# Transposing the split local probabilities by VectorE and DMAs through DRAM

## The chip, the cores and the metric

One core of a Trainium2 chip runs the whole program. The metric is the device time of one execution in microseconds (us); the time of a kernel is the median of its runs. The core has a matrix engine (TensorE, PE in the profile, with its weight loads as PEld), three engines for elementwise work (VectorE or DVE, ScalarE or ACT, GpSimd or POOL) and SP, which in this program only issues DMAs. Each engine takes its instructions in the order in which they stand in its row; between the rows semaphores order the work.

## What is computed

Eight sequences of 512 tokens, each with 32 global tokens, go through attention with 8 heads of 64 columns, and the result through a gated feed-forward network (FFN). A local token attends to the 32 global tokens and to the local ones at most 32 positions away. A global token attends to all 544.

```python
k_all = np.concatenate([k_g, k_l], axis=2)
v_all = np.concatenate([v_g, v_l], axis=2)
out_g = np.matmul(sm(scale * np.matmul(q_g, k_all.transpose(0, 1, 3, 2))), v_all)
mask = np.abs(pos[:, None] - pos[None, :]) <= 32
s_ll = np.where(mask, scale * np.matmul(q_l, k_l.transpose(0, 1, 3, 2)), -1000000000.0)
s_lg = scale * np.matmul(q_l, k_g.transpose(0, 1, 3, 2))
out_l = np.matmul(sm(np.concatenate([s_lg, s_ll], axis=-1)), v_all)
x = np.concatenate([out_g, out_l], axis=2)   # as (8 * 544) x 512
gate = 1.0 / (1.0 + np.exp(-(x @ w_gate)))
return (gate * (x @ w_val) @ w_out).astype(np.float32)
```

`sm` is the softmax over the last axis; `w_gate` and `w_val` are 512 x 1536, `w_out` is 1536 x 512.

## The kernel before

**Number format.** The matrix products keep float32 accuracy by splitting: a tensor is cast to `float32r` (the high part), the high part is subtracted from it (the low part), and a product is made from high times high, low times high and high times low. ScalarE makes the casts, GpSimd or VectorE the subtractions.

**The two streams.** `ffn_stream` (L370) emits the FFN, chunk after chunk: two chunks of 256 tokens, seven of 512 and one for the global tokens. Each of a chunk's 12 items has 12 products into `bank_g`, 12 into `bank_v` and 12 into the four output banks, in groups of four 512-column products. After each group it yields, which is one step of the clock `now`. `att_events` (L428) lays the attention of a chunk on this clock as events with due times, and the main loop (L526 to L529) emits each event when its time has come. A 512-token chunk has 108 groups, and in them runs the attention of the next chunk: 8 heads, 12 groups apart, the first `BASE` = 3 groups after the start of the chunk.

**A head.** It has two local units of two blocks of 128 queries each and one global unit, `PER` = 4 groups apart. `load_qk` (due 16 groups ahead) and `load_v` load `qk_raw` and `v_raw`, `split_qk` (10 ahead) casts `qk_raw` to `qk_hi` on ScalarE and makes the key's low part `kl` and the query's low part (in place) on GpSimd (L183 to L186). `qk_raw` has one buffer, `qk_hi` and `kl` two.

**A local unit** (`local_unit`, L211) is a generator whose parts come 0, 3, 6 and 9 groups after its due time (`STAGES`, L39):

1. scores of both blocks into one PSUM bank (L229, each block high by high and high by low), the row maximum and mask on VectorE (L241), the exponential and its sum on ScalarE (L244). The window of a block has 192 or 224 columns. The unit of blocks 2 and 3 also has the global tokens' scores among themselves (L223).
2. the reciprocal of the sum and the scaling (L252 to L255, L208)
3. the transpose of the probabilities by TensorE: four products with the identity, two a block (L264, L265: columns 0 to 127, and the last 128), into one more PSUM bank, then the split: the cast from PSUM to `pt` by ScalarE (L274) and the subtraction by VectorE (L275)
4. the products with the values (L294, L295), the sum of their parts (L297 to L299)

Units of the first two chunks and of half the third are `native`: they have no split (24 of 128 units; 104 are split).

**What sets the order.** The code hands instructions to a scheduler in the order of the events, and it makes the row of each engine, moving an instruction back where its inputs or buffers are not ready by its own estimate. In the kernel before the products of nearly all units stand 9 groups behind their scores in TensorE's row, as the due times ask. PSUM has four banks under the tag `att`, which scores, transposes, products, `bank_g` and `bank_v` share in turn. All DMAs go through SP's one row: the loads, `wo` (the split `w_out`, one load an item, two buffers, L405) and the results (`out_dram`, L423, from `ob`).

**The start.** The first chunk's units are mixed with matmuls on constants (`warm`, L199) that nobody reads.

## Time and profile before

| | us |
|---|---|
| median of 3 runs (lowest, highest) | 1208.36 (1205.93, 1217.74) |
| profiled execution | 1206.77 |
| its span, first to last instruction | 1204.7 |
| mean granted TensorE clock | 0.987 |

The profile is one execution. A span is shared out over engines and lines; a busy time counts an engine's instructions, whether or not another engine waits for them. What TensorE's share means is read from the starts of its instructions, since the ends of matmuls are modelled. The stretches of 128 us below are about one batch's FFN each, with the attention of the next batch in it up to 1033 us (columns: stretch, its length, busy time and count of PE, PEld, DVE, ACT and POOL, granted clock, busy share of the DMA engines, GB/s):

```profile
0.00:60.00 60.00, 51.97 (x318) 39.49 (x318) 41.03 (x136) 42.07 (x118) 20.22 (x35) 1.00 0.72 248
60.00:160.00 100.00, 86.23 (x514) 67.71 (x515) 74.22 (x189) 71.65 (x190) 42.39 (x35) 0.85 0.69 230
...
520.00:648.00 128.00, 127.49 (x700) 106.02 (x699) 85.76 (x280) 89.18 (x201) 72.16 (x78) 1.00 0.38 114
...
1033.00:1150.00 117.00, 117.00 (x535) 95.89 (x534) 26.39 (x49) 37.86 (x73) 24.69 (x24) 1.00 0.21 72
```

The first 160 us, with the conversion of the weights in them, have TensorE's gaps and a lower clock; from there to the end it is busy nearly without a gap, and the DMA engines are a third busy.

### The profile page before, as it was taken

The page shows a single profiled execution, that of the slowest core. Times are in us where ns is not written, and L with a number is a line of the kernel's source. Part 1 is how long each engine was busy: PE and PEld are TensorE (multiplying, and loading weights), DVE is VectorE, ACT ScalarE, POOL GpSimd, SP SyncE. Part 2 cuts the span into 40 slices and gives each one's busy share as a digit, 9 for nine tenths or more (in the row PEclk, how much of TensorE's full clock was granted, in tenths as well). Part 3 has the DMA queues.
Part 4 walks back from the last instruction along what each step waited for, and adds up shares of the span by engine and source line. Part 5 has one row for each costly group of instructions (what it writes and reads, how often), then busy time and mean ns, then how long its engine had stood idle before and what let it go on. Part 6 is the DMA issues. An engine that isn't in the chain of part 4 may idle for free.

```text
span 1204.7 us, 19673 instructions
## 1 busy us (share of the span) xinstructions
PE 1172.4 (97%) x6606; PEld 971.4 (81%) x6606; DVE 727.5 (60%) x2275; ACT 780.2 (65%) x1836; POOL 585.4 (49%) x631
## 2 busy tenths in 40 slices
PE   8887999999999999999999999999999999999998
PEld 7565778888888888888888888888888888888897
DVE  5866874756776567756765677757775677511121
ACT  6766786767677677767766767767776776532232
POOL 2442553645656366545656465636654565311111
PEclk9978899999999999999999999999999999999999
DMA  7674763433334433333334433443434332131143
GB/s 259 237 270 166 253 210 105 118 120 112 98 103 130 125 105 123 97 127 105 115 97 123 125 95 110 127 128 100 128 97 127 106 114 75 53 105 55 68 145 119
DMA packets 50277, 152.80 MB, mean 127 GB/s; under 512 B 6144, under 2 KB 7168, under 8 KB 50176
## 3 DMA queue, kind: packets, MB, share of 16 engines
q1 hardware_dynamic: 50176, 151.54, 40.2%
q8 instruction: 52, 0.85, 0.3%
q14 instruction: 49, 0.40, 0.1%
HBM read 136.31 MB, written 15.20 MB: 126 GB/s over the span
## 4 chain that ended last, share of the span: by engine, by line
PE 75%; ACT 8%; DVE 7%; issue 6%; POOL 2%; DMA 1%; SPq 0%; POOLq 0%; ACTq 0%; DVEq 0%
PE bank_g L385 20%; PE bank_o L414 19%; PE bank_v L385 18%; PE bank_x L229 5%; PE bank_x L330 3%; PE bank_x L294 2%; PE bank_y L264 2%; PE bank_y L265 2%; PE bank_x L295 2%; ACT s_buf L244 1%; PE bank_x L308 1%; DVE s_buf L208 1%; ACT pg_buf L343 1%; POOL hh L401 1%; PE bank_x L288 1%
## 5 line engine op out<-in xcount | busy, mean ns | idle before, releaser
L385 PE MATMUL bank_g<-xt,wg 128*128 128x512 f32 (+1 forms) x1440 | 337.2, 369 | 1.0 <-ACT xt L367 0.9
L385 PE MATMUL bank_v<-xt,wv 128*128 128x512 f32 (+1 forms) x1440 | 329.1, 364 | 0.0
L414 PE MATMUL bank_o<-wo,hh 128*128 128x512 f32 x1224 | 325.0, 399 | 0.3 <-ACT hh L400 0.2
L385 PEld LDWEIGHTS bank_g<-xt,wg 128*128 128x128 f32 x1440 | 239.6, 191 | 41.6 <-issue 3.0
L385 PEld LDWEIGHTS bank_v<-xt,wv 128*128 128x128 f32 x1440 | 236.3, 188 | 38.0 <-issue 1.1
L414 PEld LDWEIGHTS bank_o<-wo,hh 128*128 128x128 f32 x1224 | 219.2, 189 | 41.7 <-issue 1.1
L401 POOL TENSOR_TENSOR hh<-th,hh 128x512 fp32r<-128x512 f32 (+1 forms) x120 | 136.7, 1139 | 237.8 <-ACT hh L400 226.8
L397 DVE SCALAR_TENSOR_TENSOR bank_v<-ex,bank_v 128x512 f32<-128x512 f32 (+1 forms) x120 | 73.1, 610 | 152.1 <-PE bank_v L385 148.7
L184 POOL TENSOR_TENSOR kl<-qk_raw,qk_hi 128x736 fp32r<-128x736 f32 x52 | 92.2, 1773 | 132.9 <-ACT qk_hi L183 131.8
L244 ACT ACTIVATE s_buf<-s_buf,nm 128x192 f32<-128x192 f32 (+1 forms) x248 | 114.1, 461 | 50.2 <-DVE nm L241 47.8
L400 ACT CAST hh<-th 128x512 fp32r<-128x512 f32 (+1 forms) x120 | 66.6, 555 | 115.4 <-DVE th L398 114.7
L393 ACT ACTIVATE th<-bank_g 128x512 f32<-128x512 f32 (+1 forms) x120 | 63.4, 528 | 83.5 <-PE bank_g L385 82.6
L241 DVE CUSTOM_DVE_ANT_0 s_buf<-bank_x,masks 128x192 f32<-128x192 f32 (+1 forms) x248 | 82.3, 367 | 41.9 <-PE bank_x L229 40.4
L299 POOL TENSOR_TENSOR x<-t 64x256 f32<-64x256 f32 x104 | 77.0, 740 | 62.0 <-DVE t L298 59.4
L196 POOL TENSOR_TENSOR vhl<-v_raw,vhl 128x512 fp32r<-128x512 f32 x52 | 67.0, 1288 | 47.8 <-ACT vhl L195 45.8
L208 DVE TENSOR_SCALAR s_buf<-s_buf,r 128x224 f32<-128x224 f32 (+1 forms) x230 | 86.1, 396 | 3.8
L183 ACT CAST qk_hi<-qk_raw 128x1280 fp32r<-128x1280 f32 x52 | 65.8, 1266 | 29.1 <-PE bank_x L308 17.8
L275 DVE TENSOR_TENSOR pt<-bank_y,pt 128x512 fp32r<-128x512 f32 x104 | 71.5, 687 | 20.6 <-ACT pt L274 20.0
L298 DVE TENSOR_TENSOR t<-bank_x,t 64x512 f32<-64x512 f32 x104 | 70.7, 680 | 21.0 <-ACT t L297 17.3
L186 POOL TENSOR_TENSOR qk_hi<-qk_raw,qk_hi 64x256 fp32r<-64x256 f32 x104 | 78.8, 772 | 4.7
L252 DVE TENSOR_SCALAR r<-sm 128x2 f32<-128x2 f32 x128 | 33.5, 262 | 78.2 <-ACT s_buf L244 78.2
L398 DVE SCALAR_TENSOR_TENSOR th<-th,bank_v 128x512 f32<-128x512 f32 (+1 forms) x120 | 72.4, 603 | 6.1 <-DVE bank_v L397 0.5
(117 smaller groups left out, 2003.1 us busy)
## 6 DMA issues: line engine op xcount, KB each, us to landing
wo<-wo_dram SPq DMA_DIRECT2D x116, 512.0 KB, 3.3
qk_raw<-in_qk_dram SPq DMA_DIRECT2D x104, 320.0 KB, 4.6
v_raw<-in_v_dram SPq DMA_DIRECT2D x52, 256.0 KB, 2.6
out_dram<-ob SPq DMA_DIRECT2D x34, 256.0 KB, 3.0
xt<-in_w_gate_dram SPq DMA_DIRECT2D x12, 512.0 KB, 4.5
xt<-in_w_val_dram SPq DMA_DIRECT2D x12, 512.0 KB, 4.1
xt<-in_w_out_dram SPq DMA_DIRECT2D x12, 512.0 KB, 4.2
v_nat<-in_v_dram SPq DMA_DIRECT2D x8, 512.0 KB, 3.9
```

Of the source, the lines that this page charges most:

```text
L184: nc.gpsimd.tensor_tensor(kl, t[:, K0:Q1], hi[:, K0:Q1].bitcast(F32), op=ALU.subtract)
L186: nc.gpsimd.tensor_tensor(hi[64:128, r], t[64:128, r], hi[64:128, r].bitcast(F32), op=ALU.subtract)
L208: nc.vector.tensor_scalar(out, in_, by, None, op0=ALU.mult)
L241: anchor[0] = nc.vector.tensor_tensor_reduce(out=s_sb[:, i, 0:w], in0=s_ps[:, i, 0:w], in1=masks[:, m:m + w], scale=-0.125, scalar=3.0e38, ...
L244: nc.scalar.activation(s_sb[:, i, 0:w], s_sb[:, i, 0:w], AF.Exp, bias=nm[:, i:i + 1], scale=-1.0, accum_out=sm[:, i:i + 1])
L275: nc.vector.tensor_tensor(pt[:, 1], pt_ps, pt[:, 0].bitcast(F32), op=ALU.subtract)
L299: nc.gpsimd.tensor_tensor(dst, t0[:, :, 0], t0[:, :, 1], op=ALU.add)
L385: nc.tensor.matmul(acc, w[a][:, t, fs], xt[:, c, t, x0:x0 + ntok], start=n == 0, stop=n == 11)
L397: nc.vector.scalar_tensor_tensor(acc, ex, 1.0, acc, op0=ALU.min, op1=ALU.mult)
L398: nc.vector.scalar_tensor_tensor(th, th, 1.0, acc, op0=ALU.add, op1=ALU.mult)
L401: nc.gpsimd.tensor_tensor(hh[:, 1, 0:ntok], th, hh[:, 0, 0:ntok].bitcast(F32), op=ALU.subtract)
L414: nc.tensor.matmul(o_ps[t], ph[:, a, t * P:(t + 1) * P], pwo[:, c], start=f2 == 0 and i == 0, stop=f2 == NF - 1 and i == 2)
```

## The change

The 104 split units no longer use TensorE for step 3. VectorE transposes each 32x32 block of the two blocks' 224 columns (`tb`: 7 column blocks, 2 query blocks, 32 columns). Four DMAs, one for each 32 partitions, write it to a scratch in DRAM, `pd`, in runs of 64 numbers (256 bytes). Two DMAs read it back as 128 rows of 256 numbers each: rows 0 to 127 of the window, and rows 96 to 223. The result lies in SBUF, in the place of the low part; ScalarE casts it to the high part, and the subtraction, in place, goes to GpSimd for a head's first unit (blocks 0 and 1) and to VectorE for its second. The products read the same numbers, in runs of 32 columns.

The due times follow: writes stay at 3 groups, the reads come 5.5 groups behind them, the cast and subtraction 9, the products 11.5 (14.5 after the scores, which was 9), and `BASE` goes from 3 to -2, so that attention starts 5 groups earlier. For `ob` there are three buffers instead of four, and the warm-up uses the identity alone, twice as many products of half as many columns.

```diff
-BASE, PER = 3, 4
+BASE, PER = -2, 4
 STAGES = (0, 3, 6, 9)
+STAGES_DMA = (5.5, 9, 11.5)
...
-            nc.tensor.matmul(bank[:, 0:256], ident_r, masks_r, start=True, stop=True)
+            nc.tensor.matmul(bank[:, 0:P], ident_r, ident_r, start=True, stop=True)
...
-            s_sb = ffn.tile([P, 2, WIN], F32, name="s_first", tag="ob", bufs=4)
+            s_sb = ffn.tile([P, 2, WIN], F32, name="s_first", tag="ob", bufs=3)
...
-            pt = att.tile([P, 2, 4, P], F32R, name="pt", bufs=2)
-            nc.scalar.copy(pt[:, 0], pt_ps)
-            nc.vector.tensor_tensor(pt[:, 1], pt_ps, pt[:, 0].bitcast(F32), op=ALU.subtract)
+            tb = att.tile([P, 7, 2, 32], F32, name="tb", bufs=2)
+            pd = dram.tile([7, 32, 4, 64], F32, name="pd", bufs=3)
+            nc.vector.transpose(tb.rearrange("p b k i -> p k b i"), s_sb.rearrange("p k (b i) -> p k b i", i=32))
+            for a in range(4):
+                rows = slice(32 * a, 32 * a + 32)
+                nc.sync.dma_start(pd[:, :, a].rearrange("b j r -> j b r"), tb[rows].rearrange("p b k i -> p b (k i)"))
+            yield
+            pt = att.tile([P, 2, 2, 4, 2, 32], F32R, name="pt", bufs=2)
+            for m in range(2):
+                src = pd[3 * m:3 * m + 4].rearrange("b j a r -> (b j) (a r)")
+                nc.sync.dma_start(pt[:, 1, m].rearrange("p a k i -> p (a k i)").bitcast(F32), src)
+            yield
+            flat = pt.rearrange("p c m a k i -> p c (m a k i)")
+            nc.scalar.copy(flat[:, 0], flat[:, 1].bitcast(F32))
+            (nc.vector if blocks[0] else nc.gpsimd).tensor_tensor(
+                flat[:, 1], flat[:, 1].bitcast(F32), flat[:, 0].bitcast(F32), op=ALU.subtract)
...
-            nc.tensor.matmul(o_ps[:, i], vt[:, VM[j], :], pt[:, :, 2 * i, :], start=True, stop=False)
-            nc.tensor.matmul(o_ps[:, i], vt[0:sides[i], VS[j], :], pt[0:sides[i], :, 2 * i + 1, :], start=False, stop=True)
+            out = o_ps[:, i].rearrange("p c (a i) -> p c a i", i=32)
+            nc.tensor.matmul(out, vt[:, VM[j], :], pt[:, :, 0, :, i, :], start=True, stop=False)
+            nc.tensor.matmul(out, vt[0:sides[i], VS[j], :], pt[0:sides[i], :, 1, :, i, :], start=False, stop=True)
...
-                            ob = ffn.tile([P, DM], F32, name="ob", bufs=4)
+                            ob = ffn.tile([P, DM], F32, name="ob", bufs=3)
...
+            steps = STAGES if T["native"] else (0, 3) + tuple(3 + o / sc for o in STAGES_DMA)
```

The rows of the engines change with it. In the changed kernel L308 and L309 are the products that were L294 and L295, L399 and L428 the FFN's. TensorE's row in the steady part, before: the products of a unit (of values `vhl` and probabilities `pt`), a group of four FFN products, the transposes of another unit, a group.

```order
L294 MATMUL bank_x<-pt,vhl 128x256
L295 MATMUL bank_x<-pt,vhl 128x256
L294 MATMUL bank_x<-pt,vhl 128x256
L295 MATMUL bank_x<-pt,vhl 128x256
L385 MATMUL bank_v<-xt,wv_119 128x512 x4
L264 MATMUL bank_y<-ident,s_buf_108 128x128
L265 MATMUL bank_y<-ident,s_buf_108 128x128
L264 MATMUL bank_y<-ident,s_buf_108 128x128
L265 MATMUL bank_y<-ident,s_buf_108 128x128
L385 MATMUL bank_v<-xt,wv_118 128x512 x4
```

And in the changed kernel: the products of a head's first unit, right behind them the scores of the next head's second unit (L223 stands in front of those alone), then FFN groups and the products of the second unit.

```order
L308 MATMUL bank_x<-pt,vhl 128x256
L309 MATMUL bank_x<-pt,vhl 128x256
L308 MATMUL bank_x<-pt,vhl 128x256
L309 MATMUL bank_x<-pt,vhl 128x256
L223 MATMUL bank_x<-qk_hi 32x32
L223 MATMUL bank_x<-kl,qk_hi 32x32
L229 MATMUL bank_x<-qk_hi 128x224
L229 MATMUL bank_x<-kl,qk_hi 128x224
L229 MATMUL bank_x<-qk_hi 128x192
L229 MATMUL bank_x<-kl,qk_hi 128x192
L399 MATMUL bank_g<-xt,wg_114 128x512 x4
L399 MATMUL bank_g<-xt,wg_115 128x512 x4
```

The transposes are gone from the row, the products stand 12 to 19 groups behind their unit's scores, and a head's first product has the next head's second scores at its back.

SP's row over two heads, before: only loads (`qk_raw` and `v_raw` of a head to come, `wo` of an FFN item).

```order
L159 DMA qk_raw<-in_qk_dram 64x1280 x2
L405 DMA wo<-wo_dram_124 128x1024
L174 DMA v_raw<-in_v_dram 128x512
L159 DMA qk_raw<-in_qk_dram 64x1280 x2
L405 DMA wo<-wo_dram_125 128x1024
```

SP's row for one head and the start of the next in the changed kernel: the writes of both units, the loads of `qk_raw`, the reads of the first unit, `wo`, the reads of the second.

```order
L278 DMA pd<-tb 32x7x64 x8
L159 DMA qk_raw<-in_qk_dram 64x1280 x2
L283 DMA pt<-pd 128x256 x2
L419 DMA wo<-wo_dram_120 128x1024
L283 DMA pt<-pd 128x256 x2
L174 DMA v_raw<-in_v_dram 128x512
L278 DMA pd<-tb 32x7x64 x4
```

The loads of `qk_raw` and the first unit's reads moved behind the second unit's writes, which wait for VectorE.

GpSimd's row for a head, before: the split of the queries and keys of a head to come in one piece (`kl`, then `qk_hi` twice), then the FFN's low part `hh`.

```order
L184 TENSOR_TENSOR kl<-qk_raw,qk_hi 128x736
L186 TENSOR_TENSOR qk_hi<-qk_raw,qk_hi 64x256
L186 TENSOR_TENSOR qk_hi<-qk_raw,qk_hi 64x288
L401 TENSOR_TENSOR hh<-th,hh 128x512
L360 TENSOR_TENSOR ptg<-ptg_buf,ptg 128x5x32
```

In the changed kernel (L287 is the subtraction in `pt`, L313 the last sum of a unit's result):

```order
L184 TENSOR_TENSOR kl<-qk_raw,qk_hi 128x736
L287 TENSOR_TENSOR pt<-pt 128x512
L186 TENSOR_TENSOR qk_hi<-qk_raw,qk_hi 64x256
L186 TENSOR_TENSOR qk_hi<-qk_raw,qk_hi 64x288
L313 TENSOR_TENSOR x_5325<-t_5521 64x256
```

The subtraction of a head's first unit came in behind the `kl` of a head to come, which needs the `qk_raw` just loaded.

More of the change, by code (lines that the diff above doesn't have):

```diff
@@ L83 @@
     nc.scalar.copy(masks[:, WIN + P + 32:WIN + 192], masks[:, P + 64:WIN])
-    ident_r, masks_r = (const.tile([P, w], F32R, name=nm) for w, nm in ((P, "ident_r"), (256, "masks_r")))
+    ident_r = const.tile([P, P], F32R, name="ident_r")
     nc.scalar.copy(ident_r, ident)
-    nc.scalar.copy(masks_r, masks[:, 0:256])
     s_bufs = [const.tile([P, 2, WIN], F32, name=f"s_buf{i}") for i in range(3)]
@@ L216, in local_unit @@
         if T["first"]:
-            warm(s_ps.rearrange("p a c -> p (a c)"), 16 if h == 0 else 2)
+            warm(s_ps.rearrange("p a c -> p (a c)"), 32 if h == 0 else 4)
         with_gg = T["with_g"] and blocks[-1] == 3
@@ L255, in local_unit @@
             scaled(nat, s_sb[:, i, 0:KWIN[j]], s_sb[:, i, 0:KWIN[j]], r[:, i:i + 1])
-        yield
-        if T["first"]:
-            pt_ps = ps.tile([P, 4, P], F32, name="bank_y", tag=f"bank_o{h % 2}")
-            warm(pt_ps.rearrange("p a c -> p (a c)"), 2)
-        else:
-            pt_ps = ps.tile([P, 4, P], F32, name="bank_y", tag="att", bufs=4)
         sides = [KWIN[j] - (WIN - P) for j in blocks]
-        for i in range(2):
-            nc.tensor.transpose(pt_ps[:, 2 * i], s_sb[:, i, 0:P], ident)
-            nc.tensor.transpose(pt_ps[:, 2 * i + 1], s_sb[:, i, WIN - P:WIN], ident)
         if nat:
+            yield
+            if T["first"]:
+                pt_ps = ps.tile([P, 4, P], F32, name="bank_y", tag=f"bank_o{h % 2}")
+                warm(pt_ps.rearrange("p a c -> p (a c)"), 4)
+            else:
+                pt_ps = ps.tile([P, 4, P], F32, name="bank_y", tag="att", bufs=4)
+            for i in range(2):
+                nc.tensor.transpose(pt_ps[:, 2 * i], s_sb[:, i, 0:P], ident)
+                nc.tensor.transpose(pt_ps[:, 2 * i + 1], s_sb[:, i, WIN - P:WIN], ident)
             if T["first"] and h % 2:
@@ L272, in local_unit @@
         else:
-            pt = att.tile([P, 2, 4, P], F32R, name="pt", bufs=2)
-            nc.scalar.copy(pt[:, 0], pt_ps)
-            nc.vector.tensor_tensor(pt[:, 1], pt_ps, pt[:, 0].bitcast(F32), op=ALU.subtract)
+            tb = att.tile([P, 7, 2, 32], F32, name="tb", bufs=2)
[9 more added lines that the diff above has]
+                nc.sync.dma_start(pt[:, 1, m].rearrange("p a k i -> p (a k i)").bitcast(F32), src)
+            yield
+            flat = pt.rearrange("p c m a k i -> p c (m a k i)")
+            nc.scalar.copy(flat[:, 0], flat[:, 1].bitcast(F32))
+            (nc.vector if blocks[0] else nc.gpsimd).tensor_tensor(
+                flat[:, 1], flat[:, 1].bitcast(F32), flat[:, 0].bitcast(F32), op=ALU.subtract)
         yield
@@ L464, in att_events @@
             ev.append((base - sc * SPLIT_V, 1, lambda T=T: split_v(T)))
+            steps = STAGES if T["native"] else (0, 3) + tuple(3 + o / sc for o in STAGES_DMA)
             for i in range(npu):
                 t0 = base + per * i
-                for o in STAGES if i < nu else (0, 3, 3.9) if T["native"] else (0, 3):
+                for o in steps if i < nu else (0, 3, 3.9) if T["native"] else (0, 3):
                     ev.append((t0 + sc * o, 2, lambda h=h, i=i: adv(h, i)))
             if h % 2 == 1:
-                ev.append((base + (nu - 1) * per + sc * STAGES[-1] + 0.5, 3,
+                ev.append((base + (nu - 1) * per + sc * steps[-1] + 0.5, 3,
                            lambda kt=h // 2: x_split(xts[ci], x32s[kt], kt, x0, ntok)))
```

## The prediction

> **What bounds the kernel now.** I read the page first: the busy shares, then the chain that ended last.
>
> ```profile
> PE 1172.4 (97%) x6606; PEld 971.4 (81%) x6606; DVE 727.5 (60%) x2275; ACT 780.2 (65%) x1836; POOL 585.4 (49%) x631
> ...
> PE 75%; ACT 8%; DVE 7%; issue 6%; POOL 2%; DMA 1%; SPq 0%; POOLq 0%; ACTq 0%; DVEq 0%
> PE bank_g L385 20%; PE bank_o L414 19%; PE bank_v L385 18%; PE bank_x L229 5%; PE bank_x L330 3%; PE bank_x L294 2%; PE bank_y L264 2%; PE bank_y L265 2%; PE bank_x L295 2%; ACT s_buf L244 1%; PE bank_x L308 1%; DVE s_buf L208 1%; ACT pg_buf L343 1%; POOL hh L401 1%; PE bank_x L288 1%
> ```
>
> TensorE is idle for 32 us of 1204.7 us, so its instructions are the time: two lines of transposes, L264 and L265, hold 4% of the chain. Since a busy PE here is modelled, I then looked at start times in a steady stretch (start, duration, engine, line).
>
> ```profile
> 599.73 0.87 PE L385 MATMUL bank_g<-xt,wg 128*128 128x512 f32 x3
> 600.44 0.27 PE L264 MATMUL bank_y<-ident,s_buf 128*128 128x128 f32 x1
> 600.55 0.27 PE L265 MATMUL bank_y<-ident,s_buf 128*128 128x128 f32 x1
> 600.66 0.27 PE L264 MATMUL bank_y<-ident,s_buf 128*128 128x128 f32 x1
> 600.76 0.27 PE L265 MATMUL bank_y<-ident,s_buf 128*128 128x128 f32 x1
> 600.79 1.19 PE L385 MATMUL bank_g<-xt,wg 128*128 128x512 f32 x4
> 601.82 1.09 PE L385 MATMUL bank_v<-xt,wv 128*128 128x512 f32 x4
> 602.75 0.25 PE L229 MATMUL bank_x<-qk_hi 128*128 128x192 f32 x1
> ...
> 603.19 1.10 PE L385 MATMUL bank_v<-xt,wv 128*128 128x512 f32 x4
> 604.13 0.28 PE L294 MATMUL bank_x<-pt,vhl 128*128 128x256 f32 x1
> 604.24 0.28 PE L295 MATMUL bank_x<-pt,vhl 128*128 128x256 f32 x1
> 604.36 0.28 PE L294 MATMUL bank_x<-pt,vhl 128*128 128x256 f32 x1
> 604.48 0.28 PE L295 MATMUL bank_x<-pt,vhl 96*128 96x256 f32 x1
> ...
> 617.47 0.25 PE L229 MATMUL bank_x<-qk_hi 128*128 128x192 f32 x1
> ```
>
> A group of four FFN matmuls takes 604.13 - 603.19 = 0.94 us. From 599.73 to 601.82 seven of them and four transposes take 2.09 us; less 7 x 0.235 that leaves 0.44 us for a unit's transposes. One head (two local units and a global one among twelve groups) takes 617.47 - 602.75 = 14.72 us.
>
> **What goes.** 104 units lose their transposes: 104 x 0.44 = 46 us of TensorE. If all else hides, 1206.8 (the profiled execution; the median of the runs, 1208.4, is 1.6 us above it) becomes 1161. A head would then take 14.72 - 2 x 0.44 = 13.84 us.
>
> **What comes, engine by engine.**
>
> ```profile
> L401 POOL TENSOR_TENSOR hh<-th,hh 128x512 fp32r<-128x512 f32 x84 | 108.5, 1292 | 171.4 <-ACT hh L400 164.9 <-DMA qk_raw<-in_qk_dram 5.1
> L184 POOL TENSOR_TENSOR kl<-qk_raw,qk_hi 128x736 fp32r<-128x736 f32 x52 | 92.2, 1773 | 132.9 <-ACT qk_hi L183 131.8 <-ACT xg L311 1.1
> L275 DVE TENSOR_TENSOR pt<-bank_y,pt 128x512 fp32r<-128x512 f32 x104 | 71.5, 687 | 20.6 <-ACT pt L274 20.0
> L298 DVE TENSOR_TENSOR t<-bank_x,t 64x512 f32<-64x512 f32 x104 | 70.7, 680 | 21.0 <-ACT t L297 17.3
> L183 ACT CAST qk_hi<-qk_raw 128x1280 fp32r<-128x1280 f32 x52 | 65.8, 1266 | 29.1 <-PE bank_x L308 17.8 <-PE bank_x L330 10.9
> L357 DVE STREAM_TRANSPOSE ptg_buf<-pg_buf 32x128 f32<-32x128 f32 x208 | 62.8, 302 | 3.4
> L297 ACT COPY t<-bank_x 64x512 f32<-64x512 f32 x104 | 59.7, 574 | 2.0 <-PE bank_x L295 0.6
> L354 DVE STREAM_TRANSPOSE ptg_buf<-pg_buf 32x32 f32<-32x32 f32 x52 | 10.5, 201 | 4.1 <-ACT pg_buf L343 2.3
> ```
>
> VectorE: the block transpose has 448 columns. From 32 to 128 columns the rows grow by 101 ns, 1.05 ns a column, so about 0.64 us: 104 x 0.64 = 67 us. The subtraction (0.69 us) stays there for 52 units, so VectorE changes by 67 - 36 = +31 us, to some 63% of the span. GpSimd gets 52 subtractions of 1.29 us, +67 us. ScalarE's copy reads SBUF in place of PSUM, about the same. None of these is the bound as a sum.
>
> SP gets six DMAs a unit, 624 in all, and the DMA engines 1152 packets a unit (896 of 256 bytes, 256 of 1 KB), 50 MB.
>
> ```profile
> DMA packets 50277, 152.80 MB, mean 127 GB/s; under 512 B 6144, under 2 KB 7168, under 8 KB 50176
> ...
> q1 hardware_dynamic: 50176, 151.54, 40.2%
> ```
>
> That is 40.2% x 16 x 1204.7 us / 50176 = 154 ns for a mean packet of 3.0 KB. No row has data packets of 256 bytes. By bytes they add 50/151.5 x 40.2 = 13% of the engines' time; at the mean packet's price 119,808/50176 x 40.2 = 96%. I take 25%, near the byte end, since the mean packet is twelve times as large.
>
> The Trainium skill ("DMA: Bandwidth & Descriptors", Specifications) says that transfers under 512 B are done by read-modify-write and miss line rate. No run here shows it. By that rule the 256-byte writes lie nearer the other end, which is the second rival.
>
> **The wait that I think decides.** On TensorE the scores of a head's second unit stand right behind the product of the head before's first unit (the order under the change). Those scores feed the transpose on VectorE, this feeds four writes on SP, and behind them in SP's row stand the two loads of `qk_raw`, then the reads of `pt`. On GpSimd, `kl` (from that `qk_raw`) stands ahead of the first unit's subtraction, for which TensorE waits. So each product waits for the one before it through a loop over five engines and DRAM. First VectorE's part of it in a steady stretch, then SP's issues (start, time of issue), then `qk_raw` from issue to landing, its median and its spread:
>
> ```profile
> 608.57 0.37 DVE L241 CUSTOM_DVE_ANT_0 s_buf<-bank_x,masks 128x224 f32<-128x224 f32 x1
> ...
> 610.92 0.57 DVE L208 TENSOR_SCALAR s_buf<-s_buf,r 128x224 f32<-128x224 f32 x2
> ```
>
> ```profile
> 533.63 2.04 SPq L423 DMA_DIRECT2D out_dram<-ob  x4
> ...
> 602.56 0.34 SPq L174 DMA_DIRECT2D v_raw<-in_v_dram  x1
> 604.44 1.11 SPq L159 DMA_DIRECT2D qk_raw<-in_qk_dram  x2
> ```
>
> ```profile
> qk_raw<-in_qk_dram SPq DMA_DIRECT2D x104, 320.0 KB, 4.6
> ```
>
> ```profile
> DMA to landing us min/median/max: 3.6/4.6/7.6
> ```
>
> - product on TensorE, 604.13 to 604.76: 0.63
> - its copy and sum (L297, L298), which VectorE does ahead of the next reduction: 1.25
> - reduction to scaled probabilities, 608.57 to 611.49: 2.92
> - block transpose: 0.64
> - four issues: 1.3 (v_raw's 0.34 each) to 2.0 (the four stores); I take 1.7
> - `qk_raw`: its second issue starts 0.55 later and lands 4.6 after that (3.6 at least): 5.15
> - cast, `kl`, subtraction: 1.27 + 1.77 + 1.29 = 4.33
>
> The writes wait for the transpose on SP, and `wo` is queued behind them too:
>
> ```profile
> SPq L405 <- PE bank_o L414: 416.2, 78, 11.5
> ```
>
> SP sits waiting for a free `wo` buffer up to 11.5 us, so `wo` has slack for that; `qk_raw` is the load in the loop. Behind a product that waits, TensorE's FFN groups wait as well, since it takes its row in order.
>
> Sum of the loop: 16.6 us, against 13.84 us of TensorE's work in a head of twelve groups; with the shortest rows 15.2.
>
> Counted in the order, the groups from second scores to first product are 13, 12, 15, 9, 12.25, 14.75, 12 and 9 for the eight heads of a batch: 14.8, 13.8, 16.7, 11.0, 14.1, 16.4, 13.8 and 11.0 us. Five heads (second to sixth) have the full loop; the first, seventh and eighth have no `kl` close ahead, which leaves some 12.5 us (14 in the first, behind the stores). TensorE then lacks 2.8 (second), 5.6 (fourth), 2.5 (fifth), 0.2 (sixth) and 1.5 us (eighth): 12.6 a batch, 76 us over the six batches that run so.
>
> A wait that long also costs clock. Before (start, duration, and the idle time ahead in brackets; then a stretch with its granted clock behind the busy times):
>
> ```profile
> 107.11 0.43 PE L348 MATMUL bank_y<-ident,pg_buf 32*128 32x32 f32 x4 [2.80 <-ACT pg_buf L343]
> ...
> 121.57 0.63 PE L348 MATMUL bank_y<-ident,pg_buf 32*128 32x32 f32 x4 [2.92 <-ACT pg_buf L343]
> ```
>
> ```profile
> 120.00:130.00 10.00, 8.43 (x48) 7.83 (x49) 7.65 (x13) 6.14 (x16) 6.42 (x5) 0.66 0.84 275
> ```
>
> Around gaps of 2.8 and 2.9 us the clock falls to 0.66 over ten us, 3.4 us of full speed lost. The fourth head's 5.6 us exceeds both. Its 3.4 us go into a head that lacked 2.5 us anyway, so I add 0.9 x 6 = 5 us.
>
> The Trainium skill ("TensorE: Matmul & The Clock Gate", Part 1) puts the drop at an idle window of about 3.4 us. The trace agrees in kind. By the skill's figure the second head's 2.8 us trips nothing and the sum below stands; by the trace's gaps it is at the edge, and if it trips each time the sum is 6 x 3.4 = 20 us more, 1262.
>
> **Small edits.** The warm-up matmuls keep their columns (16 x 256 = 32 x 128) but double their loads, and a ScalarE copy ahead of them goes: between minus 3 and plus 8 us at the start, taken as nothing. Three `ob` tiles for four: the fourth result waits for the first store, with some 7 us until its bank is written again; nothing, and at most 3 us a batch if the stores land late. The products read `pt` in runs of 32 columns: taken at the 0.12 us that L294 has; twice that would add 104 x 0.47 = 49 us. Attention starts 5 groups earlier and ends half a group later, with some 6 groups left before its batch is read: nothing.
>
> Sum: 1206.8 - 46 + 76 + 5 = 1242.
>
> **Rivals.**
> 1. *It hides, and the gain comes: 1161.* The loop is shorter than I add up, since its durations overlap (VectorE has the reduction done before the sum, `qk_raw` lands before ScalarE is free). It decides where the loop falls under 13.8 us for most heads. Speaks for it: engines at 49 to 65%. Against: the shortest rows still give 15.2.
> 2. *The loop takes the shortest rows: 1201.* At 15.2 us the heads lack 1.4, 4.2, 1.1 and 0 us, 6.7 x 6 = 40.
> 3. *The small writes clog the queues: 1340.* At 77 ns a packet, half the mean, a unit's writes hold each engine 56 x 0.077 = 4.3 us, and `qk_raw` behind them lands some 3 us later. At 19.6 us the heads lack about 30 us a batch: 1161 + 180. It decides from about 40 ns a packet. For it: packets under 512 B are only counters now, so nothing shows them cheap.
> 4. *The products slow down: 1210,* 1161 + 49, with the loop hidden. No row has runs of 32.
>
> **Numbers.** Forecast 0.40 (its own range 1215 to 1290), rival 1 0.22, rival 2 0.18, rival 3 0.13, rival 4 0.07. The range 1165 to 1320 leaves out most of rival 3 and half of rival 1. One per cent, 12 us, is what a measurement of this kernel can tell from no change. Faster by more: rival 1 and a third of rival 2, with a little of rival 4, 0.29. Within: the rest of rivals 2 and 4, 0.16. Slower: 0.55.
>
> **What would show it.** Right: TensorE's share falls from 97% to about 91%; it waits ahead of the products, for GpSimd's and VectorE's `pt`, most in the fourth head; SP waits for the transposes; a head takes some 15 to 16 us. Wrong: no wait on `pt` and a head of 13.8 us (rival 1); landings of `pt` and `qk_raw` over 7 us and the DMA share near 80% (rival 3); the products' starts 0.2 us apart (rival 4).

## The result, and the profile after

The changed kernel takes 1526.47 us (median of four runs, 1522.94 to 1530.13), the kernel before 1208.96 (1205.93 to 1217.74): 1.259 times as long, 95% interval 1.251 to 1.267. The forecast was 1242 us, between 1165 and 1320.

From the page of the changed kernel: the busy shares, what its DMA queue moved, the chain that ended last by engine, then three groups of instructions (line, engine, operation, count, then busy time, mean ns, and the idle time ahead with what ended it).

```profile
PE 1265.9 (83%) x6236; PEld 1041.9 (68%) x6236; DVE 764.8 (50%) x2327; ACT 788.5 (52%) x1835; POOL 666.8 (44%) x683
...
q1 hardware_dynamic: 179968, 202.70, 44.8%
...
PE 36%; POOL 20%; issue 18%; ACT 10%; DVE 10%; DMA 3%; SPq 1%; POOLq 0%; DVEq 0%; ACTq 0%
...
L308 PE MATMUL bank_x<-pt,vhl 128*128 128x256 f32 x208 | 78.0, 386 | 218.8 <-POOL pt L287 218.8
...
L287 DVE TENSOR_TENSOR pt<-pt 128x512 fp32r<-128x512 f32 x52 | 52.5, 1009 | 62.6 <-ACT pt L286 62.6
...
L287 POOL TENSOR_TENSOR pt<-pt 128x512 fp32r<-128x512 f32 x52 | 77.0, 1480 | 5.8 <-ACT pt L286 5.6
```

The span grew by 1521.1 - 1204.7 = 316.4 us. TensorE's idle time went from 1204.7 - 1172.4 = 32.3 to 1521.1 - 1265.9 = 255.2 us, 222.9 more, nearly all of it ahead of the products, which wait for `pt`'s low part. Its busy time grew by 93.5 us, though 370 fewer instructions run on it: the mean granted clock fell from 0.987 to 0.881. In a stretch of twenty us in the steady part the clock is the number behind the five busy times, then the DMA share and GB/s:

```profile
520.00:540.00 20.00, 16.11 (x73) 13.64 (x74) 9.54 (x30) 7.81 (x20) 10.96 (x11) 0.83 0.44 120
```

Where a wait comes from is read between the first products of one head and of the next, in TensorE's row (the wait in brackets) and in the chain (start, duration, engine, what; only the longer pieces of it; it begins with the unit's third product).

```profile
701.07 0.58 PE L308 MATMUL bank_x<-pt,vhl 128*128 128x256 f32 x1 [6.32 <-POOL pt L287]
...
726.35 0.58 PE L308 MATMUL bank_x<-pt,vhl 128*128 128x256 f32 x1 [5.63 <-POOL pt L287]
```

```profile
701.87 0.21 PE bank_x L308
...
702.38 0.99 PE bank_x L229 x4
...
704.49 5.71 issue
...
710.22 1.29 POOL hh L415
...
711.60 0.74 POOL x L313
...
712.36 0.62 ACT xt L381
712.98 0.75 ACT pg_buf L353 x2
...
714.17 0.76 ACT pg_buf L357
...
716.45 0.36 DVE s_buf L241
...
716.85 1.02 ACT s_buf L244 x4
...
718.90 0.66 DVE tb L275
...
719.94 1.72 DMA pd<-tb
...
721.67 1.16 POOL hh L415
...
722.88 1.74 POOL kl L184
724.62 1.68 POOL pt L287
...
726.35 0.58 PE bank_x L308
```

From the first product at 701.07 to the first at 726.35 this is 25.3 us, where a head took 14.7. The product at 726.35 waits for a subtraction on GpSimd, which stands behind `kl`; ahead of these come a transpose, an exponential and a reduction of the next head's first unit, and ahead of that the softmax of the global tokens (`pg_buf`). None of it computes anything for this product; it stands ahead of the product's own steps in the rows of ScalarE, VectorE and GpSimd. (The 5.71 us that the chain puts down to nothing are, by the rows, FFN work: twelve products into `bank_v` from 703.16 to 707.98, VectorE's two steps on them to 709.44, ScalarE's cast to 710.09. The chain puts the start of the second `hh` down to the writes, but `hh` reads none of them; ScalarE's part of it ended at 721.59, by the row further down.) When was the data there? SP's issues of the reads, and ScalarE's row in the same head:

```profile
709.86 2.02 SPq L283 DMA_DIRECT2D pt<-pd  x4
```

```profile
716.85 0.46 ACT L244 ACTIVATE s_buf<-s_buf,nm 128x192 f32<-128x192 f32 x1
...
720.97 0.62 ACT L414 CAST hh<-th 128x512 fp32r<-128x512 f32 x1 [1.47 <-DVE th L412]
721.49 1.25 ACT L183 CAST qk_hi<-qk_raw 128x1280 fp32r<-128x1280 f32 x1
722.65 1.13 ACT L286 CAST pt<-pt 128x512 fp32r<-128x512 f32 x2
```

The landing of these reads, and of the writes and `qk_raw` (median us from issue to landing, last), and ScalarE's whole waiting for them in the run (us, times, longest):

```profile
qk_raw<-in_qk_dram SPq DMA_DIRECT2D x104, 320.0 KB, 4.1
pt<-pd SPq DMA_DIRECT2D x208, 128.0 KB, 3.7
pd<-tb SPq DMA_DIRECT2D x416, 56.0 KB, 1.7
```

```profile
ACT pt L286 <- DMA pt<-pd: 0.2, 1, 0.2
```

The reads, all issued by 709.86 + 2.02 = 711.88, had landed by about 715.6, at the median of 3.7 us; the cast began at 722.65, behind `hh` and `qk_hi`. In the whole run ScalarE waited for the reads once, for 0.2 us. The trip through DRAM is over long before anybody looks at what it brought.

### The profile page after: what moved, and what is told of

Same layout as the page of the kernel before. It is cut to its first block, busy times and chain, and to the rows that moved or that the text cites. A ratio compares the mean times of both kernels' runs of the same rounds, so it can differ in the third digit from the quotient of the medians.

```text
span 1521.1 us, 20317 instructions
## 1 busy us (share of the span) xinstructions
PE 1265.9 (83%) x6236; PEld 1041.9 (68%) x6236; DVE 764.8 (50%) x2327; ACT 788.5 (52%) x1835; POOL 666.8 (44%) x683
## 4 chain that ended last, share of the span: by engine, by line
PE 36%; POOL 20%; issue 18%; ACT 10%; DVE 10%; DMA 3%; SPq 1%; POOLq 0%; DVEq 0%; ACTq 0%
PE bank_g L399 9%; PE bank_v L399 7%; POOL hh L415 5%; PE bank_o L428 5%; POOL pt L287 4%; POOL kl L184 4%; PE bank_x L229 4%; PE bank_x L308 3%; DMA pd<-tb 3%; DVE ptg_buf L371 3%; PE bank_x L344 2%; PE bank_x L309 2%; ACT pg_buf L357 2%; POOL x L313 1%; ACT pg_buf L353 1%
## 5 line engine op out<-in xcount | busy, mean ns | idle before, releaser
L399 PE MATMUL bank_g<-xt,wg 128*128 128x512 f32 (+1 forms) x1440 | 353.4, 393 | 6.4 <-POOL xt L382 5.1
L399 PE MATMUL bank_v<-xt,wv 128*128 128x512 f32 (+1 forms) x1440 | 346.2, 385 | 0.9 <-DVE nm L241 0.9
L428 PE MATMUL bank_o<-wo,hh 128*128 128x512 f32 x1224 | 320.1, 402 | 7.9 <-ACT hh L414 5.2
L399 PEld LDWEIGHTS bank_g<-xt,wg 128*128 128x128 f32 x1440 | 268.6, 211 | 60.1 <-POOL xt L382 7.6
L399 PEld LDWEIGHTS bank_v<-xt,wv 128*128 128x128 f32 x1440 | 258.2, 204 | 46.4 <-issue 1.4
L428 PEld LDWEIGHTS bank_o<-wo,hh 128*128 128x128 f32 x1224 | 226.1, 191 | 61.4 <-ACT hh L414 8.6
L308 PE MATMUL bank_x<-pt,vhl 128*128 128x256 f32 x208 | 78.0, 386 | 218.8 <-POOL pt L287 218.8
L308 PEld LDWEIGHTS bank_x<-pt,vhl 128*128 128x128 f32 x208 | 52.2, 251 | 240.1 <-POOL pt L287 238.2
L313 POOL TENSOR_TENSOR x<-t 64x256 f32<-64x256 f32 x104 | 84.2, 810 | 264.1 <-DVE t L312 260.5
L311 ACT COPY t<-bank_x 64x512 f32<-64x512 f32 x104 | 60.4, 581 | 237.8 <-PE bank_x L309 237.3
L411 DVE SCALAR_TENSOR_TENSOR bank_v<-ex,bank_v 128x512 f32<-128x512 f32 (+1 forms) x120 | 73.5, 613 | 155.5 <-PE bank_v L399 151.5
L287 DVE TENSOR_TENSOR pt<-pt 128x512 fp32r<-128x512 f32 x52 | 52.5, 1009 | 62.6 <-ACT pt L286 62.6
L287 POOL TENSOR_TENSOR pt<-pt 128x512 fp32r<-128x512 f32 x52 | 77.0, 1480 | 5.8 <-ACT pt L286 5.6
```

The source lines that it names most:

```text
L287: (nc.vector if blocks[0] else nc.gpsimd).tensor_tensor(flat[:, 1], flat[:, 1].bitcast(F32), flat[:, 0].bitcast(F32), op=ALU.subtract)
L308: nc.tensor.matmul(out, vt[:, VM[j], :], pt[:, :, 0, :, i, :], start=True, stop=False)
L313: nc.gpsimd.tensor_tensor(dst, t0[:, :, 0], t0[:, :, 1], op=ALU.add)
L399: nc.tensor.matmul(acc, w[a][:, t, fs], xt[:, c, t, x0:x0 + ntok], start=n == 0, stop=n == 11)
L411: nc.vector.scalar_tensor_tensor(acc, ex, 1.0, acc, op0=ALU.min, op1=ALU.mult)
L428: nc.tensor.matmul(o_ps[t], ph[:, a, t * P:(t + 1) * P], pwo[:, c], start=f2 == 0 and i == 0, stop=f2 == NF - 1 and i == 2)
```

## The experiments

Every run is one execution beside one of the kernel before on the same chip (1206.6 to 1222.5 us, on different chips); a difference of some 10 us says nothing.

**Does GpSimd's subtraction make the wait?** Both subtractions on VectorE:

```diff
-            (nc.vector if blocks[0] else nc.gpsimd).tensor_tensor(
+            nc.vector.tensor_tensor(
```

> Edit: the first unit's subtraction goes to VectorE as well, so that it no longer stands behind kl in GpSimd's row. Theory A (the products wait because pt's cast and subtraction stand behind other work in the rows of ScalarE and GpSimd): kl (1.73 us) and the difference of the two subtractions (1.70 against about 0.9) leave the loop, some 2.5 us in each of 46 waits, 115 us, and some of the half-speed clock with them: 1526 falls to 1340 to 1430. Theory B (the way through DRAM is the long link): only the faster subtraction counts, 46 x 0.8 = 37 us: 1480 to 1500.

1443.3 us, 83 less, just above the upper end of theory A's range. GpSimd's row had been the last link. A next one stands close behind it: the products still wait, by the profile, 56.9 us for VectorE's subtraction and 91.8 us for nothing that it shows.

**The side edits alone.** The kernel before with `BASE` = -2, three `ob` buffers and the new warm-up:

> Edit: the kernel before with the side edits alone (BASE -2, three ob tiles, warm-up by the identity), transposes on TensorE as they were. Both theories: no change, 1200 to 1220. If the side edits hold part of the loss, above 1230.

1269.8 us. I had costed these at nothing; they are a fifth of the loss. Three runs took them one at a time.

> The kernel before with BASE = -2 and nothing else; transposes on TensorE, warm-up and ob as before. The side edits together took 1269.8 us beside 1209.5. If the earlier start of each batch's attention is what costs, this takes 1235 to 1270 us, with the marks of the batches' stores more than 3 us further apart than the 130.7 us of before. If the third ob buffer or the warm-up is the cause, it takes 1203 to 1216 us.

> The kernel before with three ob buffers in place of four and nothing else. If the stores' buffer is what costs (SP's wo load and the next store stand behind a store that waits for ob), this takes 1235 to 1270 us. If it is the earlier base or the warm-up, it takes 1203 to 1216 us. What this run and the one with the base leave of the 60 us is the warm-up's.

> The kernel before with the warm-up of the changed kernel (twice as many matmuls of 128 columns in place of those of 256) and nothing else. In the profiles of both, 32 of 128 columns took 7.09 us and 16 of 256 took 3.78, and the scores after them take 1.75 us up to 27 us where they take 0.97 from 9 us on in the kernel before. If the warm-up is what the side edits leave after the base (60 less 31 us), this takes 1228 to 1245 us, all of it before the first chunks are done; if the rest is an interplay of base and buffer, 1205 to 1215 us.

`BASE` alone 1240.6 us beside 1209.2, `ob` alone 1207.6 beside 1209.2, the warm-up alone 1238.9 beside 1206.6: 31, nothing and 32 us, which add up to the 60 or so. What the warm-up does is seen in TensorE's first rows, of the kernel before and of the run with the warm-up alone:

```profile
3.37 3.78 PE L202 MATMUL bank_x<-masks_r,ident_r 128*128 128x256 f32 x16 [3.37 <-ACT masks_r L87]
7.08 1.62 PE L229 MATMUL bank_x<-qk_nat 64*128 64x192 f32 x4
8.62 0.50 PE L202 MATMUL bank_x<-masks_r,ident_r 128*128 128x256 f32 x2
9.05 0.97 PE L229 MATMUL bank_x<-qk_nat 64*128 64x192 f32 x4
```

```profile
2.38 7.09 PE L202 MATMUL bank_x<-ident_r 128*128 128x128 f32 x32 [2.38 <-ACT ident_r L86]
9.39 1.75 PE L229 MATMUL bank_x<-qk_nat 64*128 64x192 f32 x4
...
12.12 1.75 PE L229 MATMUL bank_x<-qk_nat 64*128 64x192 f32 x4
```

One matmul of 128 columns takes 7.09/32 = 0.22 us, one of 256 columns 3.78/16 = 0.24 us: twice the number is nearly twice the time, for the same columns. And the scores behind it go on at 1.75 us where before the second set already took 0.97. In the run with the warm-up alone they still take 1.75 at 47.70 us, and 0.97 only from 56.57 on; Some 45 us at about half the pace are the larger part of the 32, by my estimate. When the pace doubles changes from run to run: with this warm-up the first set at 0.97 comes between 28.50 us (the changed kernel) and 56.57. With 256 columns of the identity it came at 6.06 us in one run below and at 26.38 in another, so it isn't shown that the width alone decides. The profile's granted clock doesn't tell this: it reads 1.00 over the first 40 us of the changed kernel.

**Is it the trip through DRAM?** The reads take a constant scratch, so that they wait for no write (left out: that dependence, and the unit's own values):

```diff
+    pd_old = dram.tile([7, 32, 4, 64], F32, name="pd_old")
...
-                src = pd[3 * m:3 * m + 4].rearrange("b j a r -> (b j) (a r)")
+                src = pd_old[3 * m:3 * m + 4].rearrange("b j a r -> (b j) (a r)")
```

> Edit: the reads of pt take a scratch that is written once at the start, so that they wait for no write of their unit (the probabilities that reach the products are constants; transposes, writes and reads are all issued). Theory A: the cast and subtraction stand where they stood, behind the FFN's casts and kl: still over 1430. Theory B: the trip scores, transpose, write, read is cut, the data is there early: below 1300.

1485.8 us, 41 less; the products still wait 199.6 us for GpSimd's subtraction. Most of the wait is not the trip. What the 41 us are stays open: ScalarE waited for the reads no more than 0.2 us in the changed kernel, and the scheduler made another order here in part.

**More work for TensorE to cover it.**

```diff
         o_ps = ps.tile([P, 2, 2, P], F32, name="bank_x", tag="att", bufs=4)
+        if blocks[0] == 0:
+            warm(o_ps.rearrange("p i c q -> p (i c q)"), 48)
```

> Edit: 48 matmuls on constants ahead of each first unit's products (52 x 48, 128 columns each, 3 to 5 us a head of added work, nobody reads them), so that TensorE is busy where it waited. If the half-speed clock after the waits holds some 140 us of the loss: the granted clock comes back from 0.88 to over 0.97 and the time falls in spite of the added work, to 1350 to 1480. If the waits alone are the loss and the clock costs nothing: 1526 or more.

1600.2 us, which is in the second range, though the clock did rise, to 0.945. TensorE was busy 1487.9 us, 222 more, for 74 us of time: much of the work did go into the holes. But the scheduler also made another order with it, so this run doesn't tell order from cover.

**Is it `qk_hi` and `kl` in front?** The load of `qk_raw` ahead of the writes, its split three groups later:

```diff
-LOAD_QK, LOAD_V, SPLIT_QK, SPLIT_V = 16, 9, 10, 4
+LOAD_QK, LOAD_V, SPLIT_QK, SPLIT_V = 18, 9, 7, 4
```

> The changed kernel with LOAD_QK 18 and SPLIT_QK 7 in place of 16 and 10: the load of qk_raw stands ahead of the small writes in SP's row, and the cast qk_hi stands directly ahead of a pt cast in 1 place of ScalarE's row, where it was 32; nothing is added or taken away. Theory A (the pt casts wait in the rows of ScalarE and GpSimd behind qk_hi and kl, which wait for their own load behind the small writes): 1400 to 1470 us, and the idle time of TensorE ahead of the products, 219 us, falls under 160. Theory B (the products are placed too few groups behind the small writes whatever stands between): 1495 to 1535 us, idle time over 200.

1504.9 us, 22 less, and the products wait 207.7 us as against 218.8: theory B. By the rows, `kl` stood between the end of the cast and GpSimd's subtraction for 42.7 us in the changed kernel and stands there for 6.6 us here, but `hh` and `qk_hi` have moved into its place (20.5 us before, 46.5 here). Taking away one thing that stands ahead, the link that the prediction chose, gives little when the next one fills its place.

**More room in the order.**

> The changed kernel with the pt cast and the products due later (STAGES_DMA 5.5, 11, 14.5 from the fourth chunk on; products 15 groups behind their scores became 18), LOAD_QK 18, SPLIT_QK 7, SPLIT_V 1 and both subtractions on VectorE; the arithmetic is the same. If slack in the order is all that is lacking, the waits ahead of the products fall under 60 us, the granted clock rises over 0.95 and the time is 1230 to 1310 us (the transposes' 46 us are then a gain against the 1269.8 us of the side edits). If each hop through the rows moves out along with the products, so that the loop stays closed, it takes 1400 to 1480 us, about what both subtractions on VectorE gave alone (1443.3).

1487.6 us, just above the second range and worse than with the subtractions alone. The products wait 184.5 us for VectorE's subtraction: in VectorE's row two or three block transposes of later units now stand ahead of it beyond its own, where it had one or two, so the loop moved out with the products.

**Without cast and subtraction.**

```diff
+            nc.gpsimd.memset(pt[:, 1].rearrange("p m a k i -> p (m a k i)").bitcast(F32), 0.0)
...
-                nc.sync.dma_start(pt[:, 1, m].rearrange("p a k i -> p (a k i)").bitcast(F32), src)
+                nc.sync.dma_start(pt[:, 0, m].rearrange("p a k i -> p (a k i)").bitcast(F32), src)
...
-            nc.scalar.copy(flat[:, 0], flat[:, 1].bitcast(F32))
-            (nc.vector if blocks[0] else nc.gpsimd).tensor_tensor(
-                flat[:, 1], flat[:, 1].bitcast(F32), flat[:, 0].bitcast(F32), op=ALU.subtract)
```

> The changed kernel without pt's cast and subtraction: the DMA writes straight into the high part, and GpSimd fills the low part with zeros before the data comes (left out: the split of the probabilities, so the products use them unsplit). TensorE's row stays as it is: of 88 products looked at, 49 stand directly behind another unit's scores, as in the changed kernel. Theory A (the products wait because the cast and the subtraction stand in the rows of ScalarE, GpSimd and VectorE behind the next units' steps, not for the transport): the idle time ahead of the products, 219 us, falls under 90, the granted clock rises over 0.93 and the time falls to 1290 to 1370 us, more than the 10 us or less a head that the two operations take. Theory B (the writes and reads through DRAM take the time, or the products' place does): 1430 to 1500 us, the products now waiting over 150 us for DMA.

And the same with the reads from a constant scratch:

> The changed kernel without cast and subtraction (the products use the probabilities unsplit, the low part is zero) and with the reads taken from a constant scratch (left out: the dependence of the reads on the writes; the values are not those of the unit). Theory A (what remains of the loss is rows, base, warm-up and clock): 1325 to 1353 us. Theory B (the transport is what remains): 1220 to 1290 us, the kernel before with the side edits less up to 46 us.

1353.4 and 1353.8 us. The products' rows of both runs:

```profile
L305 PE MATMUL bank_x<-pt,vhl 128*128 128x256 f32 x208 | 60.4, 302 | 42.9 <-DMA pt<-pd 20.3 <-POOL hh L412 12.6 <-DVE r L252 8.6
```

```profile
L309 PE MATMUL bank_x<-pt,vhl 128*128 128x256 f32 x208 | 60.2, 302 | 42.4 <-DMA pt<-pd_old 30.2 <-POOL hh L416 8.7 <-DVE r L256 2.8
```

With the two operations away the wait ahead of the products falls from 218.8 to 42.9 us and the clock rises to 0.946: 173 us, more than half the loss. With the trip's dependence taken away as well, nothing more is gained. The products keep their place behind other units' scores, so that place alone isn't what makes them wait.

**Work, or a link?** The same two operations stay on their engines, but write to a tile that nobody reads, and the products take what the DMA wrote:

```diff
-            nc.scalar.copy(flat[:, 0], flat[:, 1].bitcast(F32))
-            (nc.vector if blocks[0] else nc.gpsimd).tensor_tensor(
-                flat[:, 1], flat[:, 1].bitcast(F32), flat[:, 0].bitcast(F32), op=ALU.subtract)
+            nc.scalar.copy(nobody, flat)
+            (nc.vector if blocks[0] else nc.gpsimd).tensor_tensor(nobody, flat, nobody.bitcast(F32), op=ALU.subtract)
```

> The changed kernel with cast and subtraction behind the reads as they are, on the same engines, but written to a tile that nobody reads: the products take the high part as the DMA wrote it and a constant low part of zeros (left out: the use of the split, so the products have the probabilities unsplit). A product now waits for its reads only. The native units have one pt tile in place of two, which may cost some us at the start. Theory A (the two cost because the product stands behind them in a closed chain through three rows): 1340 to 1385 us, near the 1353 of the run without them. Theory B (they cost as work in rows that are full at those times, whoever waits): 1440 to 1530 us.

1399.0 us, between the ranges, nearer A: 127 of the 173 us come because a product waits for the two, 46 because they are work in those rows (the first of these runs had the fills in their place). Each beside its own kernel before (1222.5 here, 1206.6 there), the two parts are 141 and 30 us. The smaller one may be less still: the one tile that nobody reads makes ScalarE wait 73.5 us for the subtraction before, which it doesn't in the changed kernel. In TensorE's row the products stand where they stood without the two operations. The product's row:

```profile
L311 PE MATMUL bank_x<-pt_all,vhl 128*128 128x256 f32 x208 | 59.6, 298 | 31.8 <-DMA pt_all<-pd 24.1 <-DVE r L254 4.2 <-DVE th L415 1.7
```

**The two operations ahead of the trip.** The split is made on the block transpose's result, on ScalarE and VectorE, and high and low parts go through DRAM together:

```diff
+            nc.scalar.copy(tb[:, :, 0], low.bitcast(F32))
+            nc.vector.tensor_tensor(low, low.bitcast(F32), tb[:, :, 0].bitcast(F32), op=ALU.subtract)
             for a in range(4):
```

> The changed kernel with the same cast and subtraction made ahead of the writes, on the result of VectorE's transpose, in place of behind the reads: the writes and reads carry both parts (twice the bytes, pieces of 512 bytes in place of 256, the same number of DMAs), and nothing stands between the reads and the products. The whole arithmetic is kept; both subtractions are VectorE's. Theory A (the place of the two operations in the rows behind the reads is what cost 173 us): 1340 to 1400 us, the waits ahead of the products under 90 us. Theory B (they cost as work, wherever they stand, or the doubled bytes do): over 1430 us.

> The same with LOAD_QK 18, SPLIT_QK 7 and the warm-up of 256 columns. The warm-up alone cost the kernel before 32 us: 30 to 50 us under the run without these two edits, so about 1300 to 1360 us. It stays slower than the kernel before, since the base (31 us alone) is kept and the product still has a DMA in its way.

1439.9 us, in theory B's range, and 1414.5 with the other two edits, a miss by 55 us. That is no more than both subtractions on VectorE gave behind the reads (1443.3): moved to the other side they are still links of the same chain, and now the trip is its last one.

```profile
L307 PE MATMUL bank_x<-pt,vhl 128*128 128x256 f32 x208 | 69.8, 340 | 115.4 <-DMA pt<-pd 112.6 <-DVE s_buf L208 2.6 <-DVE tb L278 0.2
```

The products wait 112.6 us for the reads, which start later and carry both parts (253.82 MB at a DMA share of 58.6%). The trip was free only as long as something later hid it. (`tb` has one buffer here, not two; VectorE waits 16.4 us for the writes to free it, which is in the time as well.)

**Together, and spread.** Subtractions, `qk_raw` and a warm-up of 256 columns in one kernel; then the same with earlier stages:

> The changed kernel with three edits together: both subtractions on VectorE (alone 83 us less), LOAD_QK 18 with SPLIT_QK 7 (alone 22 us less), and the warm-up with 256 columns again (the identity read twice by a stride of 0, half as many matmuls; estimated 25 us less). If they act apart, 1526 less 130 us: 1385 to 1410 us. If the three free the same wait, 1420 to 1440 us.

> The kernel with those three edits, and besides STAGES_DMA 3, 7, 9.5 from the fourth chunk on in place of 5.5, 9, 11.5 (SPLIT_V 2): the order then has 11 of 88 products directly behind another unit's scores, where it had 49, and most of the rest 1 to 6 groups behind. Theory A (what is lost is the chain from those scores through VectorE and ScalarE to the subtraction, less the groups that stand between): at 3 us less for each of about 38 products, 1290 to 1350 us if the three edits alone give about 1395. Theory B (the place does not matter, since the whole row moves out with the wait): within 20 us of the three edits alone.

1410.0 us: 116 less, of the 130 that the three would give apart. The spread order took 1526.5, against both theories. The wait of ScalarE that grew most from the one to the other, first the three edits, then the spread:

```profile
ACT th L407 <- PE bank_g L399: 78.3, 55, 3.5
```

```profile
ACT th L407 <- PE bank_g L399: 161.6, 76, 4.5
```

ScalarE stood twice as long in front of the FFN's `th`, behind which its casts are queued. How many groups lie between scores and product doesn't decide; I haven't settled which row does there.

**What are the transposes worth?** The kernel before without them, cast and subtraction reading the untransposed numbers (left out: the transposes and the last 128 columns):

> The kernel before without the transposes of the split units: the cast and VectorE's subtraction read the untransposed probabilities from SBUF (left out: the transposes, and the values of the last 128 columns; the cast, the subtraction and the products keep their sizes). If the 416 transposes are worth the 104 times 0.44 us of the forecast on TensorE, the time falls by 40 to 55 us to 1152 to 1167 us. If the waits around them take their place, it stays within 1190 to 1207 us.

1218.8 us beside 1212.9. TensorE's busy time fell, the time didn't:

```profile
PE 1137.7 (93%) x6190; PEld 928.0 (76%) x6190; DVE 741.9 (61%) x2275; ACT 788.3 (65%) x1836; POOL 587.3 (48%) x631
```

```profile
PE bank_x L296 <- ACT ex L396: 21.6, 12, 2.2
```

34.7 us of work went, and 47 us of idle time came (1217.0 - 1137.7 less 32.3), the largest piece of it ahead of the products. I see in that the transposes' time covering the steps around them; only the exchange is shown. ScalarE's cast, which waited 11.0 us for the transposes before, waits 61.7 us for VectorE's scaling there, and the products then wait for ScalarE; so the result holds for this order of the rows, and another order wasn't tried.

**What is the later place worth?**

> The kernel before, transposes on TensorE and the route through PSUM, with BASE = -2 and the products of split units due 14.5 groups behind their scores in place of 9; nothing else. BASE alone took 1240.6 us. If the later place of the products is what remains of the loss (their results t and x come later in the rows of ScalarE, VectorE and GpSimd, ahead of the casts hh and xt), this takes 1300 to 1370 us. If the place costs nothing as long as nothing waits behind a DMA, 1235 to 1255 us, and the rest of the changed kernel's loss belongs to the new route itself.

1262.9 us, 22 more than `BASE` alone: between the two ranges, nearer the lower.

## Why the prediction was wrong

**The transposes, -46 us.** TensorE's own part came to 34.7 us by the run without them, but as time it was worth nothing there. The first step that failed is the one from 1206.8 to 1161 "if all else hides": with 97% busy I took every instruction removed as time, and asked only what the change adds, not what the removed work covered. That takes rival 1 down too: the run without the transposes, with nothing put in their place, doesn't show 1161 either.

**The loop, +76 us.** The second step that failed, and the largest. A loop of that kind does decide: the products wait for `pt` (all 218.8 us for GpSimd's part), a head takes 16.5 to 25.3 us within a batch, and the idle time grew by 222.9. The sum failed in its links. It went through SP, `qk_raw`'s landing (5.15 us) and `kl`. The landing was no link: ScalarE waited for `qk_raw` 0.2 us in the whole run, and for the reads 0.2. `kl` did stand ahead of the subtraction, but the run with `qk_raw` first, in which it mostly doesn't, is only 22 us shorter. What it left out is what stands in the in-order rows between the landing and the cast: the global softmax, the next unit's exponential, `hh`. Letting no product wait for what comes behind the landing gave 127 us, taking it away 173. The head-by-head sum put the worst wait in the fourth head, and none in the first, third and seventh. The trace has 46 waits for GpSimd of up to 7.0 us in 52 heads; in one batch (679.06 to 824.82 us) they are 2.1, 6.3, 5.6, 5.4, 4.8, 4.3, none and 5.7 us. I read that as each wait delaying the scores that the next one needs.

**The clock, +5 us.** The mechanism was right, the size off. The busy time grew by 93.5 us although 34.7 us of work went: some 128 us. The side edits have 46 of them (busy 1218.8 against 1172.4 in their run); the other 82 I put down to the waits, as what is left. I priced one drop a batch, since I had one wait over the threshold a batch. With waits of 4 to 7 us in most heads, the clock was 0.83 in the stretch above. The idle window of about 3.4 us that the Trainium skill gives ("TensorE: Matmul & The Clock Gate", Part 1) would let the shorter waits pass; the trace doesn't agree there. After the wait of 2.12 us that ended at 501.87 the clock was 0.50 from 502.4 to 505.8 us, so the second head's 2.8 us of the prediction, left out by that figure, would have counted too.

**Small edits, 0 us.** Two of the four were wrong: 31 us for the base and 32 for the warm-up, whose range of -3 to +8 us assumed that half the columns take half the time. The prediction's own rows spoke against that: its transposes of 128 columns start 0.11 us apart, its products of 256 columns 0.12. `ob` was right. Products in runs of 32 (rival 4) were right as well, at full clock still 0.12 us apart:

```profile
707.82 0.28 PE L308 MATMUL bank_x<-pt,vhl 128*128 128x256 f32 x1
707.94 0.28 PE L309 MATMUL bank_x<-pt,vhl 128*128 128x256 f32 x1
```

**The small writes (rival 3).** They don't clog. The queue's time grew from 0.402 x 1204.7 x 16 to 0.448 x 1521.1 x 16, 3150 us for 129,792 packets more, 24 ns each, under the 40 from which that rival decides and near the 20 that their 51.16 MB would take at the rate before; `qk_raw` lands in 4.1 us, faster than before. From the rule on transfers under 512 B (the Trainium skill, "DMA: Bandwidth & Descriptors", Specifications) the prediction took that they lie nearer the other end (as its "second rival"; it is the third); 24 ns don't bear that out.

**The account.** Beside the kernel before: base 31, warm-up 32, later products 22, transposes 0 (6, within the noise), the product behind cast and subtraction 127, these as work 46; together 258 of 317 us. Each is one run, and the parts needn't add. The warm-up's may be some 12 us less in the changed kernel, an estimate: TensorE got to its full pace there some 25 us sooner than in the run with the warm-up alone. The other some 60 stay open. They remain where the two operations are away and no product waits for the writes: 1353.8 less 1206.6 is 147 us, of which 85 are base, warm-up and later products. So they belong to the rest of the new steps (VectorE's transposes, SP's issues) or to parts that don't add. Why the earlier base costs 31 us wasn't tried either.

## What to carry to other kernels

When a step moves to another engine, don't sum its latency over engines that are half idle: write down, for each engine that it passes, what stands ahead of it in that engine's row and what that waits for, as a chain that closes on itself takes the longest way round. Instructions taken off a fully busy engine need not be worth their time, since something may have been waiting under their cover; a run that leaves them out, with the other rows as they are, tells so before the replacement is built. Price "equal work" edits from rows of the same shape: a warm-up of the same columns in twice as many matmuls cost 32 us in its run here.

## What the runs showed of the hardware

Three things that I hadn't expected. A warm-up matmul of 128 columns took 0.22 us, as long as one of 256 (0.24), and with it TensorE stayed slow for longer, though it was busy almost all the time (scores 1.75 us at 22.71 us in the changed kernel and at 47.70 in the run with the warm-up alone, where the kernel before had 0.97 at 9 us). A wait of TensorE of only 2.12 us was followed by 3.4 us at half the clock. And 129,792 small packets cost the queue only some 24 ns each, 1.7 us from issue to landing for a write of 56 KB in pieces of 256 bytes.
